# A list scheduler with other costs, a turned order inside the values operation, and new nominal places, in a fused attention and feed-forward kernel

## The chip, the core and the metric

The kernel runs on one core of a Trainium2 chip. Its engines work side by side, each through its own queue in order: TensorE (matmuls, PE in the profile), VectorE (DVE), ScalarE (ACT), GpSimd (POOL) and SyncE (SP), which issues nearly all DMA transfers. The metric is the device time of one execution in microseconds (us), lower is better.

## The reference

Eight batches, twelve heads of width 64, a sequence of 448. Attention with a sigmoid in the place of the softmax, then a mixing over the sequence of rank 32, then a feed-forward layer of width 3072:

```python
scores = scale * np.matmul(q, k.transpose(0, 1, 3, 2)) - np.log(S)
attn = 1.0 / (1.0 + np.exp(-scores))
attn_out = np.matmul(attn, v)                    # (8, 12, 448, 64)
x = attn_out.transpose(0, 2, 1, 3).reshape(B, S, 768)
h = x.transpose(0, 2, 1) @ U @ V
u = x + h.transpose(0, 2, 1)
out = u + np.maximum(u @ w_ch1, 0.0) @ w_ch2
```

## The kernel before

**Numbers.** Inputs are 64-bit floats. The weights are brought from HBM as pairs of 32-bit words and decoded on VectorE and ScalarE, then each f32 value is split into a large and a small f16 part; a product of two such values is three f16 matmuls. Batches 0 and 1 (`b < WHOLE`) do their attention in f32 instead.

**Work.** `pair(b, p, ...)` does two heads of one batch: `scores_of` (L486 on; its matmuls have L503) writes scores of four blocks of keys for two heads, each in its own bank of PSUM; `sigmoid` (L590) and the split into parts (L611 on ScalarE, L363 on VectorE) turn them into attention; `values_of` (matmuls L514 and L518) multiplies them with the values into one bank. The keys are 3 x 128 + 64. The first three blocks are done per head, with 64 columns of output each (128\*64, L518, two heads side by side in the array). The last 64 keys of both heads lie on top of each other in one block of 128 rows, so that one full matmul (128\*128, L514) does both heads. Scores use 64 rows of the array per head (64\*128, L503), again two heads side by side.

Mixing follows (`mix`, L662 to L703, for batches 0 and 1; `mix_half`, L755 and L764, for the others), then for batches 0 to 3 the feed-forward layer: `ffn_in` (18 full matmuls, L838) and `ffn_out` (12, L858), in six units per batch. Batches 4 to 7 do theirs in two pairs at the end (`in_quad`, `out_quad`, both through `product`, L1033), with seven products in the place of eight. The sums of weights for that are made on GpSimd by `quarter_sums` (L917, L921).

**Order.** Nothing of the order is written out by hand: `Plan` takes every operation with its engine, its cost, what it reads and writes, and a nominal place `pos`. `Plan.order()` simulates the engines: at each step it looks for the engine that can start something earliest, and among the operations that can start then takes the one with the lowest `pos`. An operation's start needs its inputs (`land`, `slack` and `op[5]` are latencies between engines), its engine, the port that VectorE and GpSimd share (`port`), and a free buffer for each new tile (a bank of PSUM among them: `PS_` gives batches 2 to 7 five banks for scores, values and mixing, batches 0 and 1 four; the first pairs may take all eight). The result is emitted as each engine's queue. The constants at the head of the file place the work: `START` and `ROOM0`, `ROOM` say where the feed-forward of a batch begins (`BEGIN`), `DECODE` how far ahead of its unit a weight is decoded, `BEFORE` how far ahead of batch 0's feed-forward the attention of batch 1 starts, `VALUES` and `SECOND` where a pair's values and its second scores lie, `MIX_1` and `MIX_2` the second part of the mixing, `EV_IN` and `EV_OUT` the evictions, `A_OFF` the splitting of attention, `U_AT` and `U_STEP`, `LEAD`, `SUMS`, `STEP_K`, `STEP_I` the loads and sums for the last two pairs of batches.

Of the kernel before, what the change touches and what calls it, by code (L numbers as in the profile page):

```python
# [39 lines left out]
S = 448  # L40
# [12 lines left out]
WHOLE = 2  # L53
PLAIN = 4
LATER = [2, 4, 3, 5, 6, 7]
FORMS = {1: (0,), 2: (1,), 3: (2,)}
MM = 0.190

ROOM0, ROOM, AHEAD, BEFORE, PACE = 36.845, 45.6, 45.326, 25.79, 0.913
PREP, BOUNDS, VALUES, SECOND, MIXED = 15.498, 8, 1.44, 2.168, 6.09  # L60
LOW_POOL = ()
MIXED1, MIX_1 = 6.452, 3.6
MIX_2, EV_IN, EV_OUT, A_OFF = 6.852, 20.566, 6.028, 0.0
START, DECODE = 55.894, 39.655
U_AT, U_STEP = 4.779, 4.652
LEAD, SUMS, STEP_K, STEP_I, FFN_LEAD = 30.119, 20, 24.441, 14, 4.0
ORDER = "iiiioiooiioiooiioiooiooo"


# [19 lines left out]
class Plan:  # L89
# [10 lines left out]
        self.queues.setdefault(name, []).append(t)  # L100
        return t

    def op(self, eng, cost, fn, reads=(), writes=(), pos=0.0, slack=0.0, land=0.12, after=(), port=False):
        deps = set(after)
        for k in reads:
            deps.update(self.wrote.get(k, ()))
        for k in writes:
            deps.update(self.wrote.get(k, ()))
            deps.update(self.read.get(k, ()))
        i = len(self.ops)  # L110
        for k in reads:
            self.read.setdefault(k, []).append(i)
        for k in writes:
            self.wrote[k], self.read[k] = [i], []
        tiles = []
        for k in (*reads, *writes):
            t = k[0] if isinstance(k, tuple) else k
            if isinstance(t, Tile) and t not in tiles:
                tiles.append(t)
                t.users.append(i)  # L120
                if t.at is None:
                    t.at = (pos, i)
        self.ops.append((eng, cost, fn, sorted(deps), pos, slack, land, tiles, port))
        return i

    def order(self):
        n = len(self.ops)
        left = [len(o[3]) for o in self.ops]
        users = [[] for _ in range(n)]
        for i, o in enumerate(self.ops):  # L130
            for d in o[3]:
                users[d].append(i)
        for q in self.queues.values():
            q.sort(key=lambda t: t.at)
            for t in q:
                t.left = len(t.users)
        ready, end = [0.0] * n, [0.0] * n
        free, cand = {}, {}
        for i, o in enumerate(self.ops):
            free.setdefault(o[0], 0.0)  # L140
            cand.setdefault(o[0], [])
            if not left[i]:
                cand[o[0]].append(i)
        done, port, landed = [], 0.0, [0.0] * 8

        def room(i):

            when, taken = 0.0, []
            for t in self.ops[i][7]:
                if t.got is None:  # L150
                    if t.in_turn and self.queues[t.name][0] is not t:
                        return None
                    best = None
                    for b in t.buffers:
                        if b.live or b in taken or any(x.live for x in b.shares):
                            continue
                        at = max([b.free] + [x.free for x in b.shares])
                        if best is None or at < best[0]:
                            best = at, b
                    if best is None:  # L160
                        return None
                    taken.append(best[1])
                    when = max(when, best[0])
            return when, taken

        while len(done) < n:
            best = None
            for e, c in cand.items():
                now = []
                for i in c:  # L170
                    r = room(i)
                    if r is not None:
                        o = self.ops[i]
                        now.append((max(free[e], ready[i], r[0] + o[5] if r[1] else 0.0, port if o[8] else 0.0, landed[-8] if e == "SP" else 0.0), o[4], i))
                if now:
                    t = min(now)[0]
                    if best is None or t < best[0]:
                        best = t, e, now
            if best is None:
                raise RuntimeError(f"stuck after {len(done)} of {n}")  # L180
            t, e, now = best
            i = min((x[1], x[2]) for x in now if x[0] <= t + 1e-9)[1]
            o = self.ops[i]
            taken = room(i)[1]
            for x in o[7]:
                if x.got is None:
                    x.got = taken.pop(0)
                    x.got.live = True
                    if x.in_turn:
                        self.queues[x.name].pop(0)  # L190
            cand[e].remove(i)
            end[i] = t + o[1]
            free[e] = end[i]
            if o[8]:
                port = end[i]
            if e == "SP":
                landed.append(end[i] + o[6])
            done.append(i)
            for x in o[7]:
                x.left -= 1  # L200
                x.got.free = max(x.got.free, end[i] + o[6])
                if not x.left:
                    x.got.live = False
            for u in users[i]:
                x = self.ops[u]
                at = end[i] + (o[6] + x[5] if x[0] != e or e == "SP" else 0.0 if e == "PE" else 0.06)
                ready[u] = max(ready[u], at)
                left[u] -= 1
                if not left[u]:
                    cand[x[0]].append(u)  # L210
        return done
# [9 lines left out]
def fused_kernel(ctx: ExitStack, tc: tile.TileContext, q, k, v, wu, wv, w1, w2, out):  # L221
    nc = tc.nc
    B = q.shape[0]
    plan = Plan()
    op = plan.op
# [114 lines left out]
        op("SP", max(0.6, n / 0.30e6), lambda: nc.sync.dma_start(out=dst(), in_=src()), reads, writes, pos, land=land)  # L340

    def dve(cost, fn, reads, writes, pos):
        op("DVE", cost, fn, reads, writes, pos)

    def dve2(cost, fn, reads, writes, pos):

        op("DVE", cost, fn, reads, writes, pos, port=True)

    def act(cost, fn, reads, writes, pos):
        op("ACT", cost, fn, reads, writes, pos)  # L350

    def pool(cost, fn, reads, writes, pos, after=()):
        op("POOL", cost, fn, reads, writes, pos, after=after, port=bool(reads))

    def pe(cost, fn, reads, writes, pos, slack=0.8, after=()):
        return op("PE", cost, fn, reads, writes, pos, slack, 0.3, after)

    def ts(eng, out, in_, s1, op0, s2=None, op1=None):
        kw = {} if op1 is None else {"op1": op1}
# [112 lines left out]
    values_ops, scored, summed = [], [], []  # L472
# [13 lines left out]
    def scores_of(b, js, products, kp, pos, early):  # L486


        sc = {(j, h): plan.tile("sc", BANK if early else PS_[b], False) for j in js for h in range(2)}
        n = 1 if b < WHOLE else 3  # L490

        def fn():
            for j in js:
                for i, (x, y) in enumerate(products()):
                    for h in range(2):
                        if b < WHOLE:
                            o = sc[j, h].x[:, :S] if j < 3 else sc[j, h].x[rows_of(h), :S]
                            keys = x[rows_of(h), j * P : min(S, j * P + P)]
                        else:
                            o = sc[j, h].x[:, :S]  # L500
                            first = j * P - (D if j == 3 and h else 0)
                            keys = x[rows_of(h), first : first + P]
                        nc.tensor.matmul(o, keys, y[rows_of(h)], start=i == 0, stop=i == n - 1)  # L503

        scored.append(pe(len(js) * (4 if b < WHOLE else 3) * MM + 0.2, fn, kp, list(sc.values()), pos, after=values_ops[-2:-1]))
        return sc

    def values_of(b, products, tiles, kp, pos):
        av = plan.tile("av", PS_[b], False)

        def fn():
            n = len(products())
            for i, (x, y) in enumerate(products()):
                nc.tensor.matmul(av.x[:, :S], x[:, 3, :], y(tiles[3], 0), start=i == 0, stop=False, skip_group_check=True)  # L514
            for j in range(3):
                for i, (x, y) in enumerate(products()):
                    for h in range(2):
                        nc.tensor.matmul(  # L518
                            av.x[rows_of(h), :S], x[:, j, rows_of(h)], y(tiles[j], h),
                            start=False, stop=j == 2 and i == n - 1, skip_group_check=True,  # L520
                        )

        values_ops.append(pe((16 if b < WHOLE else 12) * MM + 0.2, fn, kp, [av], pos))
        return av

    def pair(b, p, at, d):
# [406 lines left out]
    ready = {}  # L933
# [249 lines left out]
    for n, (b, g) in enumerate(slots):  # L1183
# [3 lines left out]
        at = BEGIN[b] + g * step  # L1187
# [106 lines left out]
```

## Time and profile before

| | |
|---|---|
| median of 3 runs | 1583.21 us (1581.95 to 1583.43) |
| profiled execution, from its first to its last instruction | 1581.4 us |
| TensorE matmul busy | 1561.2 us, 99%, 8774 instructions |
| VectorE busy | 1126.2 us, 71%, 1887 instructions |
| ScalarE busy | 859.8 us, 54%, 1553 instructions |
| GpSimd busy | 362.3 us, 23%, 468 instructions |
| DMA moved | 319.37 MB, 202 GB/s on average |
| granted TensorE clock, mean | 0.996 |

The profiled execution has no other time of its own beside its span; the runs lie around it and take some 1.8 us more by their median. A matmul's recorded duration (0.35 us for 448 columns) overlaps the next one; from start to start full ones follow every 0.19 us, so starts tell more than busy time.

### The profile page before, as it was taken

The numbers are of one execution on the slowest core, as the hardware profiler recorded it, in microseconds if no ns is written. First come the engines' busy times: TensorE is split into PE (matmuls) and PEld (weight loads), VectorE is DVE, ScalarE is ACT, GpSimd is POOL, SyncE is SP. The second block draws the span as 40 slices with busy tenths as digits, with TensorE's granted clock in tenths as the row PEclk, the third lists the DMA queues.
The fourth block names the chain that finished last, engine by engine and source line by source line (L and its number), as shares of the span: only waits on it lengthen the run. The fifth ranks groups of instructions, "written<-read, shape, count | busy, mean of one in ns | idle before, by whom it ended". The sixth has DMA issues, their size and how long they took to land.

```text
span 1581.4 us, 23841 instructions
## 1 busy us (share of the span) xinstructions
PE 1561.2 (99%) x8774; PEld 767.9 (49%) x8774; DVE 1126.2 (71%) x1887; ACT 859.8 (54%) x1553; POOL 362.3 (23%) x468
## 2 busy tenths in 40 slices
PE   8999998999999999999999999999999999999999
PEld 3344444544444444444444454555555555555554
DVE  3798899667767568767667677687677677565656
ACT  7667655468867757757878758332323614131210
POOL 0100002541212533312153411045543500000000
PEclk9999999999999999999999999999999999999999
DMA  8798898885565787664666584887675663333321
GB/s 248 237 308 283 277 297 261 277 267 143 151 196 142 226 256 195 183 212 97 189 225 193 167 265 162 264 268 237 216 230 181 216 225 135 124 105 133 113 105 70
DMA packets 208724, 319.37 MB, mean 202 GB/s; under 512 B 126176, under 2 KB 174688, under 8 KB 196320
## 3 DMA queue, kind: packets, MB, share of 16 engines
q1 hardware_dynamic: 208608, 317.86, 64.5%
q8 instruction: 68, 1.11, 0.3%
q14 instruction: 48, 0.39, 0.1%
HBM read 246.25 MB, written 77.42 MB: 205 GB/s over the span
## 4 chain that ended last, share of the span: by engine, by line
PE 93%; DMA 2%; DVE 2%; ACT 1%; SPq 1%; issue 0%; ACTq 0%; DVEq 0%
PE bank L1033 36%; PE bank L838 20%; PE bank L858 19%; PE bank L503 8%; PE bank L518 5%; PE bank L514 2%; PE bank L755 1%; SPq L747 1%; DMA w<-w_in 1%; DMA forms<-xnt 0%; PE bank L382 0%; DMA v__102<-v_in 0%; PE bank L764 0%; DVE stg__108 L363 0%; SPq L340 0%; DMA parked<-ub__85 0%
## 5 line engine op out<-in xcount | busy, mean ns | idle before, releaser
L858 PE MATMUL bank<-h__94,w__92 128*128 128x448 f16 x864 | 172.6, 353 | 1.3 <-DVE ua__78 L363 1.3
L858 PE MATMUL bank<-h__93,w__91 128*128 128x448 f16 x864 | 172.9, 353 | 0.0
L363 DVE SCALAR_TENSOR_TENSOR a<-at,a 128x896 f16<-128x896 f32 (+1 forms) x145 | 142.1, 988 | 32.5 <-ACT a L611 32.1
L838 PEld LDWEIGHTS <-w__89 128*128 128x128 f16 x864 | 83.5, 98 | 83.2 <-issue 7.3
L611 ACT ACTIVATE a<-at 128x896 f16<-128x896 f32 (+1 forms) x144 | 123.2, 856 | 0.7
L858 PEld LDWEIGHTS <-w__92 128*128 128x128 f16 x864 | 82.0, 98 | 84.8 <-issue 11.5
L838 PEld LDWEIGHTS <-w__90 128*128 128x128 f16 x864 | 82.9, 98 | 82.2 <-issue 8.4
L858 PEld LDWEIGHTS <-w__91 128*128 128x128 f16 x864 | 81.6, 98 | 82.5 <-issue 10.5
L1033 PEld LDWEIGHTS <-w__89 128*128 128x128 f16 x819 | 79.9, 98 | 74.6 <-issue 0.4
L1033 PEld LDWEIGHTS <-w__91 128*128 128x128 f16 x756 | 74.0, 98 | 69.0
L1033 PEld LDWEIGHTS <-w__90 128*128 128x128 f16 x756 | 74.0, 98 | 69.0
L921 POOL TENSOR_TENSOR w<-w 128x384 f32<-128x384 f32 x96 | 103.7, 1080 | 5.1
L1033 PEld LDWEIGHTS <-w__92 128*128 128x128 f16 x693 | 67.8, 98 | 63.3
L838 PE MATMUL bank<-us__87,w__89 128*128 128x448 f16 x432 | 85.2, 353 | 1.4 <-ACT h__93 L846 1.1
L838 PE MATMUL bank<-us__87,w__90 128*128 128x448 f16 x432 | 85.8, 354 | 0.6 <-DVE ua__79 L363 0.6
L838 PE MATMUL bank<-us__88,w__90 128*128 128x448 f16 x432 | 85.5, 353 | 0.0
L838 PE MATMUL bank<-us__88,w__89 128*128 128x448 f16 x432 | 85.0, 353 | 0.0
L590 ACT ACTIVATE at<-bank,bias_s,c__226 128x448 f32<-128x448 f32 (+1 forms) x96 | 67.0, 728 | 19.3 <-PE bank L503 18.7
L590 ACT ACTIVATE at<-bank,bias_s,c__225 128x448 f32<-128x448 f32 (+1 forms) x96 | 67.0, 723 | 10.7 <-PE bank L503 5.5
L590 ACT ACTIVATE at<-bank,bias_s,c__224 128x448 f32<-128x448 f32 (+1 forms) x96 | 66.9, 724 | 5.8 <-PE bank L503 4.0
L917 POOL TENSOR_TENSOR w<-w 128x384 f32<-128x384 f16 x48 | 46.0, 986 | 98.8 <-DVE xnt L925 70.0
L917 POOL TENSOR_TENSOR w<-w__89 128x384 f32<-128x384 f16 x16 | 15.2, 973 | 206.0 <-DMA forms<-scratch 178.1
(1173 smaller groups left out, 3121.7 us busy)
## 6 DMA issues: line engine op xcount, KB each, us to landing
w<-w_in SPq DMA_DIRECT2D x48, 768.0 KB, 5.9
forms<-xnt SPq DMA_DIRECT2D x24, 768.0 KB, 4.9
w__89<-forms SPq DMA_DIRECT2D x13, 1344.0 KB, 5.7
w__90<-forms SPq DMA_DIRECT2D x12, 1344.0 KB, 6.5
w__91<-forms SPq DMA_DIRECT2D x12, 1344.0 KB, 5.8
w__92<-forms SPq DMA_DIRECT2D x11, 1344.0 KB, 5.9
forms<-scratch SPq DMA_DIRECT2D x144, 96.0 KB, 4.3
w__89<-scratch SPq DMA_DIRECT2D x9, 1536.0 KB, 8.4
```

The costliest lines, as they stand in the source:

```text
L363: nc.vector.scalar_tensor_tensor(out=out, in0=in0, scalar=s, in1=in1, op0=op0, op1=op1)
L503: nc.tensor.matmul(o, keys, y[rows_of(h)], start=i == 0, stop=i == n - 1)
L514: nc.tensor.matmul(av.x[:, :S], x[:, 3, :], y(tiles[3], 0), start=i == 0, stop=False, skip_group_check=True)
L518: nc.tensor.matmul(av.x[rows_of(h), :S], x[:, j, rows_of(h)], y(tiles[j], h), start=False, stop=j == 2 and i == n - 1, skip_group_check=True,)
L590: act(cost, lambda: nc.scalar.activation(out_(), in_(), AF.Sigmoid, bias=bias_s[rows], scale=c if whole else c.x[rows]), kin + ["bias"] + ...
L611: act(0.57 if j == 3 else 0.95, lambda a=a, to=to: nc.scalar.activation(half(a, 0), to.x, AF.Copy, scale=A_UP), kto, [(a, 0)], here + A_OFF)
L747: op("SP", 1.0, lambda: nc.sync.dma_start_transpose(out=xt.x, in_=xs.x.rearrange("p c x s -> p (c x s)")), [(xs, i, x) for i in range(3) f ...
L838: nc.tensor.matmul(ph.x[:, :S], wx[:, x, c, f * P : (f + 1) * P], us.x[:, c, y, :], start=c == 0 and i == 0, stop=c == NP - 1 and i == 2,)
L858: nc.tensor.matmul(po.x[:, :S], wx[:, x, f, e * P : (e + 1) * P], h.x[:, f, y, :], start=f == 0 and i == 0, stop=f == FC - 1 and i == 2,)
L917: pool(1.0, lambda j=j: nc.gpsimd.tensor_tensor(out=t.x[:, j], in0=quarter(j, 0), in1=quarter(j, 1), op=ALU.add), [(w, j, 0), (w, j, 1)] i ...
L921: pool(1.0, lambda o_=o_, x=x, y=y, sub=sub: nc.gpsimd.tensor_tensor(out=t.x[:, o_], in0=t.x[:, x], in1=t.x[:, y], op=ALU.subtract if sub ...
L1033: nc.tensor.matmul(bank.x[:, :S], wt.x[:, k, FACTOR[n], x], both(f)[:, y], start=start and k == i == 0, stop=k == 2 and i == 2, skip_group ...
```

## The change

Four things change together.

1. In `values_of` the three half-width blocks come first and the block with the last keys, on the full array, last. The first half-width product now opens the accumulation and the last full one closes it.
2. The scheduler keeps the array's shape (`mode`). An operation on TensorE has the shape that it starts in and the one that it leaves (`modes`): (64, 64) for scores, (32, 32) for scores of batches 0 and 1 with the last keys among them, (65, 128) for values, (128, 128) for all else. A start in another shape than the last one adds `SWITCH` = 0.11 us. While the array stands in a shape other than the full one, an operation that starts in the same shape counts as 6 us earlier (`BOND`).
3. Costs on VectorE fall by 0.08 us and on ScalarE by 0.1 us, while their latency to other engines rises by as much (0.12 to 0.20 and to 0.22); a dependent operation on the same engine follows after 0.14 us where it was 0.06. A matmul is counted as 0.1893 us where it was 0.190, and scores and values get costs of their own.
4. The constants that set nominal places are new.

```diff
-MM = 0.190
-
-ROOM0, ROOM, AHEAD, BEFORE, PACE = 36.845, 45.6, 45.326, 25.79, 0.913
-PREP, BOUNDS, VALUES, SECOND, MIXED = 15.498, 8, 1.44, 2.168, 6.09
+MM = 0.1893
+SWITCH, BOND = 0.11, 6.0
+
+ROOM0, ROOM, AHEAD, BEFORE, PACE = 29.307, 45.6, 45.326, 22.996, 0.913
+PREP, BOUNDS, VALUES, SECOND, MIXED = 15.026, 7.753, 1.44, 2.168, 6.09
 LOW_POOL = ()
-MIXED1, MIX_1 = 6.452, 3.6
-MIX_2, EV_IN, EV_OUT, A_OFF = 6.852, 20.566, 6.028, 0.0
-START, DECODE = 55.894, 39.655
-U_AT, U_STEP = 4.779, 4.652
-LEAD, SUMS, STEP_K, STEP_I, FFN_LEAD = 30.119, 20, 24.441, 14, 4.0
+MIXED1, MIX_1 = 6.452, 3.7
+MIX_2, EV_IN, EV_OUT, A_OFF = 8.978, 21.237, 6.028, 1.237
+START, DECODE = 55.894, 41.023
+U_AT, U_STEP = 4.779, 4.182
+LEAD, SUMS, STEP_K, STEP_I, FFN_LEAD = 30.453, 24.808, 24.441, 12.798, 3.912
...
-        done, port, landed = [], 0.0, [0.0] * 8
+        done, port, landed, mode = [], 0.0, [0.0] * 8, 128
...
-                        now.append((max(free[e], ready[i], r[0] + o[5] if r[1] else 0.0, port if o[8] else 0.0, landed[-8] if e == "SP" else 0.0), o[4], i))
+                        bond = BOND if e == "PE" and mode != 128 and o[9][0] == mode else 0.0
+                        now.append((max(free[e], ready[i], r[0] + o[5] if r[1] else 0.0, port if o[8] else 0.0, landed[-8] if e == "SP" else 0.0), o[4] - bond, i))
...
             end[i] = t + o[1]
+            if e == "PE":
+                end[i] += SWITCH if o[9][0] != mode else 0.0
+                mode = o[9][1]
             free[e] = end[i]
...
-                at = end[i] + (o[6] + x[5] if x[0] != e or e == "SP" else 0.0 if e == "PE" else 0.06)
+                at = end[i] + (o[6] + x[5] if x[0] != e or e == "SP" else 0.0 if e == "PE" else 0.14)
...
     def dve(cost, fn, reads, writes, pos):
-        op("DVE", cost, fn, reads, writes, pos)
+        op("DVE", max(0.06, cost - 0.08), fn, reads, writes, pos, land=0.2)
...
     def act(cost, fn, reads, writes, pos):
-        op("ACT", cost, fn, reads, writes, pos)
+        op("ACT", max(0.06, cost - 0.1), fn, reads, writes, pos, land=0.22)
...
-        scored.append(pe(len(js) * (4 if b < WHOLE else 3) * MM + 0.2, fn, kp, list(sc.values()), pos, after=values_ops[-2:-1]))
+        scored.append(pe(len(js) * (0.74 if b < WHOLE else 0.57), fn, kp, list(sc.values()), pos, after=values_ops[-2:-1],
+                         modes=(64, 64) if b >= WHOLE or js[0] < 3 else (32, 32)))
...
             n = len(products())
-            for i, (x, y) in enumerate(products()):
-                nc.tensor.matmul(av.x[:, :S], x[:, 3, :], y(tiles[3], 0), start=i == 0, stop=False, skip_group_check=True)
             for j in range(3):
                 for i, (x, y) in enumerate(products()):
                     for h in range(2):
                         nc.tensor.matmul(
                             av.x[rows_of(h), :S], x[:, j, rows_of(h)], y(tiles[j], h),
-                            start=False, stop=j == 2 and i == n - 1, skip_group_check=True,
+                            start=j == 0 and i == 0, stop=False, skip_group_check=True,
                         )
-
-        values_ops.append(pe((16 if b < WHOLE else 12) * MM + 0.2, fn, kp, [av], pos))
+            for i, (x, y) in enumerate(products()):
+                nc.tensor.matmul(av.x[:, :S], x[:, 3, :], y(tiles[3], 0), start=False, stop=i == n - 1, skip_group_check=True)
+
+        values_ops.append(pe((2.97 if b < WHOLE else 2.28) + SWITCH, fn, kp, [av], pos, modes=(65, 128)))
```

More of the change, by code (lines that the diff above doesn't have):

```diff
@@ L101, in tile, with op @@
         return t
-    def op(self, eng, cost, fn, reads=(), writes=(), pos=0.0, slack=0.0, land=0.12, after=(), port=False):
+    def op(self, eng, cost, fn, reads=(), writes=(), pos=0.0, slack=0.0, land=0.12, after=(), port=False, modes=(128, 128)):
         deps = set(after)
@@ L122, in op @@
                     t.at = (pos, i)
-        self.ops.append((eng, cost, fn, sorted(deps), pos, slack, land, tiles, port))
+        self.ops.append((eng, cost, fn, sorted(deps), pos, slack, land, tiles, port, modes))
         return i
@@ L342, in dve, with pe @@
     def dve(cost, fn, reads, writes, pos):
-        op("DVE", cost, fn, reads, writes, pos)
+        op("DVE", max(0.06, cost - 0.08), fn, reads, writes, pos, land=0.2)
     def dve2(cost, fn, reads, writes, pos):
-        op("DVE", cost, fn, reads, writes, pos, port=True)
+        op("DVE", max(0.06, cost - 0.08), fn, reads, writes, pos, land=0.2, port=True)
     def act(cost, fn, reads, writes, pos):
-        op("ACT", cost, fn, reads, writes, pos)
+        op("ACT", max(0.06, cost - 0.1), fn, reads, writes, pos, land=0.22)
     def pool(cost, fn, reads, writes, pos, after=()):
         op("POOL", cost, fn, reads, writes, pos, after=after, port=bool(reads))
-    def pe(cost, fn, reads, writes, pos, slack=0.8, after=()):
-        return op("PE", cost, fn, reads, writes, pos, slack, 0.3, after)
+    def pe(cost, fn, reads, writes, pos, slack=0.8, after=(), modes=(128, 128)):
+        return op("PE", cost, fn, reads, writes, pos, slack, 0.3, after, modes=modes)
     def ts(eng, out, in_, s1, op0, s2=None, op1=None):
```

## The prediction

> **What bounds the kernel now.** I read the page first, then the busy time by stage, then the order of time on TensorE, then its waits. The page's head, its first row and the chain's shares:
>
> ```profile
> span 1581.4 us, 23841 instructions
> ...
> PE 1561.2 (99%) x8774; PEld 767.9 (49%) x8774; DVE 1126.2 (71%) x1887; ACT 859.8 (54%) x1553; POOL 362.3 (23%) x468
> ...
> PE 93%; DMA 2%; DVE 2%; ACT 1%; SPq 1%; issue 0%; ACTq 0%; DVEq 0%
> ```
>
> TensorE sets the end nearly everywhere, and the change alters no matmul's size and no count. So only time in which TensorE streams nothing can be won: stalls, stretches at half clock, and changes of the array's shape. The stages (columns: stretch, its length, then busy us and instructions of PE, PEld, DVE, ACT, POOL, then granted clock, DMA share, GB/s) say where it is:
>
> ```profile
> 0.00:40.00 40.00, 35.89 (x148) 12.73 (x149) 12.48 (x21) 28.32 (x52) 1.40 (x11) 1.00 0.81 247
> 40.00:87.00 47.00, 43.51 (x167) 15.25 (x166) 38.99 (x80) 30.70 (x63) 10.09 (x10) 0.93 0.79 247
> 87.00:205.00 118.00, 118.00 (x603) 56.27 (x602) 105.67 (x181) 81.39 (x161) 0.00 (x0) 1.00 0.87 288
> 205.00:260.00 55.00, 48.77 (x257) 25.38 (x255) 52.36 (x101) 31.79 (x64) 0.00 (x0) 0.97 0.92 310
> 260.00:310.00 50.00, 50.00 (x271) 25.40 (x269) 38.15 (x75) 18.83 (x32) 24.32 (x35) 1.00 0.78 240
> 310.00:1000.00 690.00, 687.31 (x4275) 334.11 (x4274) 488.25 (x810) 500.16 (x896) 209.49 (x298) 1.00 0.67 195
> 1045.00:1581.00 536.00, 532.74 (x2817) 275.36 (x2814) 356.15 (x562) 152.29 (x259) 110.55 (x109) 1.00 0.50 166
> ```
>
> Idle time of TensorE, length less busy: 4.1 us until 40, 3.5 in 40 to 87, none in 87 to 205, 6.2 in 205 to 260, none in 260 to 310, 2.7 in 310 to 1000, 3.3 in the last row. The first is the load of the first q and k, the last is what follows the last matmul; no edit touches either. Two stages ran below full clock: 0.07 of 47 us is 3.3 us, 0.03 of 55 us is 1.7 us. What an edit can reach is thus 3.5 + 3.3 = 6.8 us in 40 to 87, 6.2 + 1.7 = 7.9 in 205 to 260 and 2.7 in 310 to 1000: **17.4 us**, 1.1% of the span. The waits at which most of it is lost, by TensorE in order of time, and then two from the list of waits:
>
> ```profile
> 83.53 1.02 PE L514 MATMUL bank<-a,v__105 128*128 128x448 f32 x2 [1.64 <-ACT a L590]
> ...
> 253.41 0.32 PE L684 MATMUL bank<-xnt,ua 128*128 128x384 f16 x1 [1.01 <-ACT xnt L677]
> 255.71 0.32 PE L684 MATMUL bank<-xnt,ub 128*128 128x384 f16 x1 [1.98 <-DVE xnt L363]
> ```
>
> ```profile
> PE bank L755 <- ACT ub__82 L617: 1.1, 1, 1.1
> PE bank L764 <- DVE xnt L363: 0.8, 1, 0.8
> ```
>
> In 205 to 260 VectorE is the late one: it is busy 52.36 of 55 us with the last decodes, the evictions of batch 0 and the mixing of batch 1, all in one queue.
>
> **Part one: values end with the last keys.** Within a values operation (L510 to L521) the order turns round: 18 half-width matmuls first, three full ones last. What that costs is the price of changing the array's shape, from this order on TensorE:
>
> ```profile
> 321.15 1.31 PE L503 MATMUL bank<-stg__109 64*128 64x448 f16 x12
> 322.39 3.58 PE L838 MATMUL bank<-us__88,w__90 128*128 128x448 f16 x18
> 325.81 0.73 PE L514 MATMUL bank<-a,stg__108 128*128 128x448 f16 x3
> 326.47 1.89 PE L518 MATMUL bank<-a,stg__108 128*64 128x448 f16 x18
> 328.30 1.31 PE L503 MATMUL bank<-stg__109 64*128 64x448 f16 x12
> ...
> 338.63 3.57 PE L838 MATMUL bank<-us__88,w__90 128*128 128x448 f16 x18
> 342.03 4.70 PE L858 MATMUL bank<-h__93,w__91 128*128 128x448 f16 x24
> ```
>
> Starts tell the pitch: 18 full matmuls take 342.03 - 338.63 = 3.40 us, 0.189 each. Three full ones before half-width ones take 0.66 where 0.567 is streaming: 0.09 more. Twelve scores run in pairs, so 6 x 0.189 = 1.13 is streaming and 322.39 - 321.15 = 1.24 is taken: 0.11 more. So a change of shape costs **0.1 us in either direction**. A values operation between full matmuls has two changes before (full to half, half to full) and two after. Directly behind scores it had three and will have two; directly ahead of scores it had two and will have three. In batches 2 to 7, of 36 values operations, 12 stand directly ahead of scores (the first is above, 326.47 to 328.30) and 6 directly behind; the last of the former and first of the latter:
>
> ```profile
> 968.75 1.89 PE L518 MATMUL bank<-a,stg__109 128*64 128x448 f16 x18
> 970.57 1.31 PE L503 MATMUL bank<-stg__108 64*128 64x448 f16 x12
> ```
>
> ```profile
> 381.40 1.31 PE L503 MATMUL bank<-stg__108 64*128 64x448 f16 x12
> 382.64 0.74 PE L514 MATMUL bank<-a,stg__109 128*128 128x448 f16 x3
> ```
>
> With this order kept, 12 - 6 = 6 changes are added: **+0.6 us**. What a values operation adds to the changes that its neighbours have anyway is 2 between full matmuls in both orders, 2 before and 1 after where it stands behind scores, 1 before and 2 after where it stands ahead of them: 18 x 2 + 6 x 2 + 12 x 1 = 60 now. All 36 behind scores would make 36 (-2.4 us), all ahead of them 72 (+1.2 us). I take +0.6 because VALUES and SECOND, which set who stands beside whom, are untouched. The 12 values operations of batches 0 and 1 move it by 1.2 us at most. [...]
>
> BOND lets the scheduler draw scores together. In batches 2 to 7 one scores operation fills four of the five banks that scores and values share, so a second can't follow before ScalarE has emptied them: I take nothing for it there, and less than the 0.6 us above for batches 0 and 1.
>
> **Part two: occupancy apart from latency.** VectorE operations now hold their engine 0.08 us less in the plan, ScalarE's 0.1 less, with as much added before another engine may read. Does the chip do so? VectorE from 219.40, then ScalarE:
>
> ```profile
> 219.40 0.68 DVE L363 SCALAR_TENSOR_TENSOR ua__80<-bank,kg__179,ua__80 128x448 f32<-128x448 f32 x1
> 219.99 0.95 DVE L363 SCALAR_TENSOR_TENSOR stg__109<-w,stg__109 128x768 int32<-128x768 int32 x1
> 220.86 0.55 DVE L360 TENSOR_SCALAR at<-w 128x768 int32<-128x768 int32 x1
> ```
>
> ```profile
> 324.42 0.57 ACT L611 ACTIVATE a<-at 128x448 f16<-128x448 f32 x1
> 324.89 0.72 ACT L590 ACTIVATE at<-bank,bias_s,c__225 128x448 f32<-128x448 f32 x1
> ```
>
> From start to start they take 0.59, 0.87 and 0.47 us where the old plan counted 0.68, 0.97 and 0.57: the new figures (0.60, 0.89, 0.47) are the chip's. In the stage of 87 to 205 the old plan thus counted 181 x 0.08 = 14.5 us of VectorE work that wasn't there, and there VectorE indeed idles 118 - 105.67 = 12.3 us, just ahead of the stage in which TensorE waits for it. A planner that sees these 12.3 us can put decode work there (DECODE goes from 39.7 to 41.0, the step of a unit shrinks by 1/6 of the 8.1 us by which the first batch's stretch is shorter), and 6.2 us of idle need less than that. Against a full gain: DMA is at 0.87 already, and a decode needs its loads. Bounds: 0 won to all 7.9. **I take half, -3.9 us.** In 40 to 87 the chain runs through batch 0's mixing and scaling, which follow each other whatever the order; bounds 0 to 6.8, of which I take a **quarter, -1.7**. In 310 to 1000 only single waits are left, of the kind that the moved halves of mixing (MIX_2 6.9 to 9.0) and later conversions (A_OFF 1.2) address; a **third of 2.7, -0.9**.
>
> The other side of all three bounds: a new order can put fresh waits at other places, up to as much again (the third rival prices the likeliest). After 1045 the stage has no wait; LEAD, SUMS, STEP_I and FFN_LEAD change when loads and copies are due there, under cover of 0.50 DMA share and VectorE at 66%, and I cost them at nothing; uncovered, one such load late by its own time to landing (the last column) would cost 5.7 us:
>
> ```profile
> w__89<-forms SPq DMA_DIRECT2D x13, 1344.0 KB, 5.7
> ```
>
> **Sum.** -3.9 - 1.7 - 0.9 + 0.6 = **-5.9 us**: the span goes from 1581.4 to 1575.5. The median of the runs, 1583.2, lies 1.8 above the profiled span, so the time is **1577.3 us**.
>
> **Rivals.**
> *Nothing moves*: 1583 us (1580.1 to 1586.3). For it: TensorE has no idle at all in 87 to 205 and 260 to 310, and 205 to 260 has VectorE at 95% and DMA at 0.92, so decode may have nowhere to go; a stall closed at 212 reopens at 255. Then only +0.6 of the first part is left.
> *The change does not what it says*: if scores and values never come to stand otherwise and BOND never acts, the first part alone gives 1583.8. That is inside the rival above.
> *Slower, because batch 1 is ready late*. Decode is put 1.4 us sooner and batch 1's attention starts 2.8 us later (BEFORE), so both engines may work off decodes ahead of batch 1's mixing. What decides is when batch 1's split inputs are done against when TensorE wants them:
>
> ```profile
> 289.23 0.68 DVE L363 SCALAR_TENSOR_TENSOR us__88<-ub__86,s_u__177,us__88 128x448 f16<-128x448 f32 x1
> ...
> 291.12 1.11 PE L838 MATMUL bank<-us__88,w__89 128*128 128x448 f16 x5
> ```
>
> They are done at 289.91, 1.2 us before the first chain of batch 1. Later than that by more than 1.2 us against batch 0's last chain, each us costs one us; by 8 us it is 6.8, and 1583.2 + 6.8 = **1590 us**.
>
> **How the numbers follow.** Forecast 0.50, nothing moves 0.27, slower 0.23. What a measurement can tell from no change is about 0.2%, 3.2 us: faster is below 1580.0, slower above 1586.4. The forecast's own range is 1567 (nearly all 17.4 us) to 1580; taking in the other cases but the worst of the slower one, 1567 to 1589. A little of the forecast's chance lies within 0.2%, and a little of the second rival's below: 0.50, 0.27, 0.23.
>
> **What would show it.** TensorE's idle in the stretch before batch 1's first chain falls from 6.2 to about 3 us, and its granted clock rises from 0.97; VectorE's idle in the stretch ahead shrinks from 12.3. In batches 2 to 7, values show 18 half-width matmuls, then three full ones, with 0.1 us more where scores follow. Wrong would be: a first chain of batch 1 later than 291 us with split inputs that end just before it; a stage after 1045 that shows waits; or scores standing together in batches 2 to 7, which would mean that the banks allow what I excluded.

## The result

The changed kernel takes 1588.81 us by the median of 20 runs (1581.48 to 1592.72), the kernel before 1583.13 us (20 runs, 1581.83 to 1585.77). The ratio is 1.0032 with a 95% interval of 1.0024 to 1.0040: **slower by 5 us**, where 6 us faster was forecast. The runs of the changed kernel also spread over 11 us, those of the kernel before over 4. The profiled execution is one of the longer ones: its span of 1589.2 us is 7.8 us over the one of before, so its rows show some 2 us more than the medians. The spread goes with the granted clock: in the changed kernel the eight runs with a mean clock of 1.000 have a median of 1586.0 us, and the two with 0.996, of which the profiled one is one, take 1592.2 and 1592.7.

The page of the changed kernel, head, first row and shares of the chain of waits:

```profile
span 1589.2 us, 23843 instructions
...
PE 1564.5 (98%) x8774; PEld 768.4 (48%) x8774; DVE 1131.0 (71%) x1887; ACT 854.5 (54%) x1553; POOL 367.7 (23%) x468
...
PE 78%; DMA 7%; DVE 6%; issue 3%; ACT 3%; SPq 2%; POOL 1%; ACTq 0%; POOLq 0%; DVEq 0%
```

TensorE held 93% of the chain before, and DMA 2%. Idle time of TensorE went from 1581.4 - 1561.2 = 20.2 to 24.7 us, its busy time up by 3.3: together, but for rounding, the 7.8. Most lines lie 4 to 6 further down in the changed kernel: scores are L508, half-width values L522, full values L527, `ffn_in` L844, `ffn_out` L864. Its stages, with the columns of the stage rows of before:

```profile
0.00:40.00 40.00, 35.05 (x144) 13.18 (x144) 10.43 (x14) 28.20 (x52) 1.39 (x11) 1.00 0.80 235
40.00:87.00 47.00, 44.43 (x171) 15.30 (x170) 38.54 (x80) 30.03 (x60) 6.72 (x7) 0.93 0.77 250
87.00:205.00 118.00, 115.65 (x588) 54.95 (x588) 111.43 (x193) 83.28 (x168) 2.95 (x3) 1.00 0.85 288
205.00:260.00 55.00, 54.87 (x298) 28.85 (x296) 51.73 (x100) 29.07 (x57) 2.92 (x6) 1.00 0.84 279
...
310.00:1000.00 690.00, 681.03 (x4222) 329.90 (x4222) 481.68 (x798) 486.14 (x881) 206.19 (x294) 1.00 0.68 194
1000.00:1045.00 45.00, 43.71 (x242) 21.81 (x239) 28.54 (x53) 19.03 (x34) 0.64 (x1) 1.00 0.85 278
1045.00:1589.00 544.00, 539.85 (x2853) 278.88 (x2851) 366.74 (x580) 156.72 (x265) 118.87 (x114) 1.00 0.49 165
```

Length less busy gives TensorE's idle time: in 205 to 260 it fell from 6.2 to 0.1 us, and the clock rose from 0.97 to 1.00. In 87 to 205 it rose from nothing to 2.3, in **310 to 1000 from 2.7 to 9.0**, in 1000 to 1045 from nothing to 1.3. In the last row TensorE is busy 7.1 us longer than before (539.85 against 532.74): that is work which came late to 1045, not a slower tail. The waits of TensorE, longest sums first (what waits, who released it, us in all, times, the longest):

```profile
PE bank L770 <- DVE xnt L368: 4.5, 3, 2.3
PE bank L508 <- DMA qk__99<-q_in: 4.2, 1, 4.2
PE bank L522 <- ACT a L596: 3.2, 2, 2.6
PE bank L761 <- ACT at L596: 1.9, 2, 1.6
PE bank L864 <- DVE h__93 L853: 1.2, 1, 1.2
```

The second row is the first load, as before. The waits of mixing (L770, L761) in batches 2 to 7 are the new ones: 4.5 and 1.9 us, where the list of before had 0.8 and 1.1 at the same places. Behind the longest of them the granted clock is 0.57 from 827 to 831, which by an estimate, 0.43 x 4, costs 1.7 us more that counts as busy: 12 matmuls start there, and 23 in the 4 us after it.

One of them, followed back. SyncE's queue, then ScalarE, then TensorE (start, duration, engine, line, operation; in brackets the idle time ahead and what ended it):

```profile
419.55 3.88 SPq L753 DMA_TRANSPOSE w<-w  x1
...
424.17 0.53 SPq L345 DMA_DIRECT2D qk__101<-k_in  x1
```

```profile
428.57 0.58 ACT L425 ACTIVATE junk<-qk__101 128x448 bf16<-128x448 f32 x1 [6.46 <-DMA qk__101<-k_in]
...
429.85 0.53 ACT L851 ACTIVATE r__96<-bank 128x448 f32<-128x448 f32 x1
...
430.69 0.71 ACT L596 ACTIVATE at<-bank,bias_s,c__226 64x448 f32<-64x448 f32 x1
```

```profile
427.65 2.24 PE L864 MATMUL bank<-h__93,w__91 128*128 128x448 f16 x11
431.46 0.65 PE L761 MATMUL bank<-w,ua 128*128 128x384 f16 x3 [1.56 <-ACT at L596]
```

A transfer that transposes holds SyncE's queue for 3.88 us. The load of k behind it starts at 424.17 and has landed at 428.57, when ScalarE has waited 6.46 us at the head of its queue to compute the bound of that load. The relu and the sigmoid of other work stand behind it in the same queue, and TensorE runs out of work at 429.9.

The longest of these waits has the same head, here SyncE's queue, ScalarE and TensorE:

```profile
810.04 5.08 SPq L753 DMA_TRANSPOSE w<-w  x1
...
818.94 0.58 ACT L425 ACTIVATE junk<-qk__100 128x448 bf16<-128x448 f32 x1 [4.90 <-DMA qk__100<-q_in]
...
827.33 0.55 PE L770 MATMUL bank<-vst,xnt 128*128 128x448 f16 x1 [2.30 <-DVE xnt L368]
```

The next longest, 1.70 us at 614.63, goes back to another late transfer: ScalarE stood 2.10 us for `forms<-xnt`. These three are 5.6 of the 9.0 us.

### The profile page after: what moved, and what is told of

It reads as the page before. It is cut to its first block, busy times and chain, and to the rows that moved or that the text cites. A ratio compares the mean times of both kernels' runs of the same rounds, so it can differ in the third digit from the quotient of the medians.

```text
span 1589.2 us, 23843 instructions
## 1 busy us (share of the span) xinstructions
PE 1564.5 (98%) x8774; PEld 768.4 (48%) x8774; DVE 1131.0 (71%) x1887; ACT 854.5 (54%) x1553; POOL 367.7 (23%) x468
## 4 chain that ended last, share of the span: by engine, by line
PE 78%; DMA 7%; DVE 6%; issue 3%; ACT 3%; SPq 2%; POOL 1%; ACTq 0%; POOLq 0%; DVEq 0%
PE bank L1039 35%; PE bank L864 15%; PE bank L844 15%; PE bank L508 5%; PE bank L522 4%; PE bank L527 2%; DMA w<-w_in 1%; SPq L345 1%; ACT at L596 1%; DVE a L368 1%; PE bank L761 1%; DVE stg__108 L368 1%; DMA qk__101<-q_in 1%; DVE stg__109 L368 1%; ACT junk L425 1%
## 5 line engine op out<-in xcount | busy, mean ns | idle before, releaser
L864 PE MATMUL bank<-h__93,w__91 128*128 128x448 f16 x864 | 173.5, 353 | 1.2 <-DVE h__93 L853 1.2
L864 PE MATMUL bank<-h__94,w__92 128*128 128x448 f16 x864 | 173.1, 353 | 0.0
L844 PE MATMUL bank<-us__87,w__90 128*128 128x448 f16 x648 | 130.0, 355 | 0.5 <-ACT inv_w__191 L394 0.5
L844 PE MATMUL bank<-us__87,w__89 128*128 128x448 f16 x648 | 127.7, 353 | 0.6 <-DVE us__87 L368 0.4
L844 PEld LDWEIGHTS <-w__90 128*128 128x128 f16 x864 | 83.7, 98 | 84.1 <-issue 9.2
L864 PEld LDWEIGHTS <-w__91 128*128 128x128 f16 x864 | 82.8, 98 | 83.1 <-issue 8.9
L844 PEld LDWEIGHTS <-w__89 128*128 128x128 f16 x864 | 83.1, 98 | 82.2 <-issue 6.7
L864 PEld LDWEIGHTS <-w__92 128*128 128x128 f16 x864 | 82.6, 98 | 79.9 <-issue 6.6
L617 ACT ACTIVATE a<-at 128x896 f16<-128x896 f32 (+1 forms) x144 | 117.8, 856 | 0.5
L927 POOL TENSOR_TENSOR w<-w 128x384 f32<-128x384 f32 x96 | 108.4, 1129 | 5.0
L596 ACT ACTIVATE at<-bank,bias_s,c__226 128x448 f32<-128x448 f32 (+1 forms) x96 | 64.8, 721 | 18.7 <-PE bank L508 14.7
L596 ACT ACTIVATE at<-bank,bias_s,c__225 128x448 f32<-128x448 f32 (+1 forms) x96 | 65.2, 722 | 17.7 <-PE bank L508 9.3
L596 ACT ACTIVATE at<-bank,bias_s,c__224 128x448 f32<-128x448 f32 (+1 forms) x96 | 64.7, 721 | 11.5 <-PE bank L508 6.3
L596 ACT ACTIVATE a<-bank,bias_s 128x448 f32<-128x448 f32 (+1 forms) x96 | 55.1, 640 | 3.5 <-PE bank L508 2.8
L851 ACT ACTIVATE r__95<-bank 128x448 f32<-128x448 f32 x48 | 25.9, 540 | 52.9 <-PE bank L844 49.9
L365 POOL TENSOR_SCALAR inv_qkv__218<-e_qkv__215 128x3 f32<-128x3 f32 x12 | 3.8, 313 | 204.1 <-DVE e_qkv__215 L365 200.3
```

Of the source, the lines that this page charges most:

```text
L596: act(cost, lambda: nc.scalar.activation(out_(), in_(), AF.Sigmoid, bias=bias_s[rows], scale=c if whole else c.x[rows]), kin + ["bias"] + ...
L617: act(0.57 if j == 3 else 0.95, lambda a=a, to=to: nc.scalar.activation(half(a, 0), to.x, AF.Copy, scale=A_UP), kto, [(a, 0)], here + A_OFF)
L844: nc.tensor.matmul(ph.x[:, :S], wx[:, x, c, f * P : (f + 1) * P], us.x[:, c, y, :], start=c == 0 and i == 0, stop=c == NP - 1 and i == 2,)
L851: act(0.54, lambda: nc.scalar.activation(r.x, ph.x[:, :S], AF.Relu, scale=DOWN_H), [ph], [r], pos - EV_IN)
L864: nc.tensor.matmul(po.x[:, :S], wx[:, x, f, e * P : (e + 1) * P], h.x[:, f, y, :], start=f == 0 and i == 0, stop=f == FC - 1 and i == 2,)
L927: pool(1.0, lambda o_=o_, x=x, y=y, sub=sub: nc.gpsimd.tensor_tensor(out=t.x[:, o_], in0=t.x[:, x], in1=t.x[:, y], op=ALU.subtract if sub ...
```

## The experiments

All ratios are against the kernel before, run beside it. The question of the first four was which of the parts loses the time.

**The turned values order alone.** The kernel before, with only the emission inside `values_of` turned:

```diff
-            for i, (x, y) in enumerate(products()):
-                nc.tensor.matmul(av.x[:, :S], x[:, 3, :], y(tiles[3], 0), start=i == 0, ...)
             for j in range(3):
...
+            for i, (x, y) in enumerate(products()):
+                nc.tensor.matmul(av.x[:, :S], x[:, 3, :], y(tiles[3], 0), start=False, stop=i == n - 1, ...)
```

> The kernel before with only the turned order inside the values operation; every queue's order is otherwise the same. By the count of shape changes (12 values operations ahead of scores, 6 behind them in batches 2 to 7) the time rises by 0.6 us, to 1583.8, with no new wait. Rival: values now need the block that ScalarE and VectorE finish last 0.57 us sooner, and TensorE waits at the third block: more than 2 us slower, with idle time at the half-width matmuls.

Measured: 1583.89 us, ratio 0.9998 (0.9988 to 1.0009), which is -1.9 to +1.4 us. The forecast's +0.6 lies inside, and the rival's 2 us or more lies outside.

**The scheduler alone.** New costs, shapes and bond with the old places and the old order inside values:

```diff
-MM = 0.190
+MM = 0.1893
+SWITCH, BOND = 0.11, 6.0
...
-        op("DVE", cost, fn, reads, writes, pos)
+        op("DVE", max(0.06, cost - 0.08), fn, reads, writes, pos, land=0.2)
...
+        values_ops.append(pe((2.97 if b < WHOLE else 2.28) + SWITCH, fn, kp, [av], pos, modes=(128, 65)))
```

> The kernel before with only the scheduler's new costs, shapes and bond; old order of values, old nominal places. Theory A (the new costs are to blame: the 0.08 and 0.1 us were the plan's reserve for late loads and the shared port, and without it single waits come up in 310 to 1000 us): 1586 to 1590, with 5 us or more of TensorE idle in 310 to 1000. Theory B (the new places are to blame): 1578 to 1584, idle in 310 to 1000 near the 2.7 us of before.

Measured: 1601.26 us, ratio 1.0116 (1.0098 to 1.0134). Its stage row:

```profile
310.00:1000.00 690.00, 677.24 (x4177) 326.39 (x4175) 480.31 (x799) 490.26 (x889) 201.68 (x288) 0.99 0.67 189
```

12.8 us of idle time there, more than in the whole change. Prices nearer to the chip's did not by themselves make a better order on the chip.

**The places alone.** The old scheduler with the new constants:

```diff
-ROOM0, ROOM, AHEAD, BEFORE, PACE = 36.845, 45.6, 45.326, 25.79, 0.913
+ROOM0, ROOM, AHEAD, BEFORE, PACE = 29.307, 45.6, 45.326, 22.996, 0.913
...
-MIX_2, EV_IN, EV_OUT, A_OFF = 6.852, 20.566, 6.028, 0.0
+MIX_2, EV_IN, EV_OUT, A_OFF = 8.978, 21.237, 6.028, 1.237
```

> The kernel before with only the new nominal places; old costs, old order of values. Theory A: 1581 to 1585, idle in 310 to 1000 near 2.7 us. Theory B: 1587 to 1592, with 6 us or more of idle there, at the second half of the mixing.

Measured: 1620.86 us, ratio 1.0234 (1.0220 to 1.0248). Its stages:

```profile
205.00:310.00 105.00, 90.99 (x465) 46.89 (x464) 87.36 (x164) 45.06 (x85) 26.38 (x36) 0.95 0.86 272
...
1000.00:1050.00 50.00, 38.99 (x232) 16.92 (x228) 31.79 (x55) 33.35 (x53) 6.61 (x10) 0.86 0.55 181
```

14.0 us idle where the whole change has 0.2 (205 to 310), and 11.0 in 1000 to 1050. The parts do not add: +1.2% and +2.3% alone, +0.3% together. Both theories failed at this: neither had a range above 1592 for either part. The places belong to the scheduler with which they are used.

**The whole change with the old order inside values**, and the plan told so:

```diff
-        values_ops.append(pe((2.97 if b < WHOLE else 2.28) + SWITCH, fn, kp, [av], pos, modes=(65, 128)))
+        values_ops.append(pe((2.97 if b < WHOLE else 2.28) + SWITCH, fn, kp, [av], pos, modes=(128, 65)))
```

> The whole change but for the order inside values, which stays as before (the plan is told that it starts full and ends half-width). Theories A and B both: 1588, within 1.5 us of the whole change, the difference being shape changes of 0.1 us each. If it is at 1583 or below, the turned order is what costs, by another way than the count of shape changes.

Measured: 1609.97 us, ratio 1.0164 (1.0150 to 1.0178): 22 us above the 1588 that was expected. The next run shows that it isn't the matmuls: there the plan was left as the change has it, and only the emission inside values turned back.

```diff
+            for i, (x, y) in enumerate(products()):
+                nc.tensor.matmul(av.x[:, :S], x[:, 3, :], y(tiles[3], 0), start=i == 0, ...)
             for j in range(3):
...
-            for i, (x, y) in enumerate(products()):
-                nc.tensor.matmul(av.x[:, :S], x[:, 3, :], y(tiles[3], 0), start=False, stop=i == n - 1, ...)
```

> The whole change with the plan exactly as it is (it still thinks that values start half-width and end full), but the values operation written out in the old order, full block first. 17 values operations of batches 2 to 7 stand ahead of scores and 9 behind them in this plan, so the old order has 8 changes of shape less: 0.8 us faster, 1588.0. If it is at 1584 or below, the turned order itself costs; if at 1609, as with the old order told to the plan, the order on TensorE and not the plan decides.

Measured: 1588.30 us, ratio 1.0028 (1.0015 to 1.0041), as expected and as the change itself. So the 21 us of the kernel ahead of it came from another order that the plan drew, because a values operation was declared to start and end in other shapes.

**How much does one order weigh?** The change with a single figure of the plan put back:

```diff
-MM = 0.1893
+MM = 0.190
```

> The whole change with one number of the plan put back: a matmul counted as 0.190 us instead of 0.1893. No instruction changes, only the order. Theory D with nominal places that fit one single order: the plan's own end goes from 1577.7 to 1601.3, and the chip follows, 1600 or more. If places had a meaning beyond that one order, 0.0007 us per matmul would move the time by less than 3 us: 1586 to 1592.

Measured: 1616.43 us, ratio 1.0189 (1.0169 to 1.0209). By the ratios, 0.7 ns per matmul in the plan moved the chip by some 25 us (1.6%). The plan's own end had moved as far, from 1577.7 to 1601.3: the places fit one order, and the plan saw that. Its longest wait of TensorE:

```profile
PE bank L864 <- DMA w__91<-scratch: 6.7, 1, 6.7
```

A weight that is fetched late.

**Are late loads the cause?** Two ways to take them away, each done to both kernels. First the weights that batches 1 to 3 fetch, cut from 6144 columns to 64 (12,288 bytes per partition to 128), so that less is in the way of the loads there (the DMA engines' busy share in 310 to 1000 falls from 0.68 to 0.46):

```diff
-        load(lambda: w.x, lambda: scratch[i][g], P * 2 * WE * 2, [("scratch", i, g)], kw_of(w), pos)
+        load(lambda: w.x[:, 0, :64], lambda: scratch[i][g][:, 0, :64], P * 2 * WE * 2, [("scratch", i, g)], kw_of(w), pos)
```

> The whole change, with every queue's order kept, but each of the 36 fetches of scaled weights for batches 1 to 3 moves 64 columns of its 6144 (1/96 of 1536 KB; the products then use what lies in the buffer). Theory D (loads land later than the plan says, 3 to 8 us for q and k against 2.6 planned, because these transfers are in their way, and the new plan has no reserve for it): TensorE's idle in 310 to 1000 us falls from 9 to 3 us or less and the time to 1578 to 1583. Theory E (the engines' own costs are too low in the plan): the time stays at 1587 to 1590.

> The kernel before with the same 36 fetches cut to 64 columns. It has 2.7 us of idle in 310 to 1000, so under both theories at most 3 us are won: 1580 to 1583.5. If it gains as much as the change with light weights, the transfers cost both plans alike and are not what tells them apart.

Measured: the change 1581.33 us, ratio 0.9987 (0.9977 to 0.9996); the kernel before 1581.07 us, ratio 0.9987 (0.9977 to 0.9998). Idle time of TensorE in 310 to 1000 falls from 9.0 to 2.6 us in the changed kernel, and from 2.7 to nothing in the one before; their rows in that order:

```profile
310.00:1000.00 690.00, 687.42 (x4273) 334.05 (x4272) 486.84 (x806) 491.59 (x891) 204.38 (x295) 1.00 0.46 123
```

```profile
310.00:1000.00 690.00, 690.00 (x4301) 335.92 (x4299) 490.16 (x811) 501.62 (x898) 206.63 (x298) 1.00 0.46 122
```

The two kernels then take the same time: the change gains 7 us from it and the kernel before 2. In 310 to 1000 the change still idles 2.6 us more, where it was 6.3.

Second, the 12 transposing transfers replaced by plain copies of the same bytes:

```diff
-        op("SP", 1.0, lambda: nc.sync.dma_start_transpose(out=xt.x, in_=...),
+        op("SP", 1.0, lambda: nc.sync.dma_start(out=xt.x, in_=...),
```

> The whole change, orders kept, with each of the 12 transposing transfers of the mixing replaced by a plain copy of the same bytes (the mixing then sees untransposed data). A transposing transfer holds SyncE's queue for 3.2 to 6.4 us where the plan counts 1.0, and the loads of q, k and v stand behind it. Theory D in this form (the queue, not the other transfers): 1580 to 1584. If the queue is not what delays: 1587 to 1589.

> The kernel before with the 12 transposing transfers replaced by plain copies of the same bytes, orders kept (the mixing sees untransposed data). Theory D (the new plan has no reserve for SyncE's queue being held; the old one has): at most 3 us are won, 1580 to 1583.5, against 11 us in the change. Rival (the transfers hold both kernels alike, and the change is slower for another reason): 10 us or more are won here too, 1573 or less.

Measured: the change 1577.82 us, ratio 0.9967 (0.9956 to 0.9979); the kernel before 1579.98 us, ratio 0.9964 (0.9951 to 0.9976). Equal again by the ratios: the change gains 10 us from it (0.65%), the kernel before 6 us (0.36%). Both gains are larger than expected: 1580 to 1584 was the range for the change, and at most 3 us for the kernel before. So the transfers cost both kernels something, and the change more by nearly all that it is slower. Their rows, in the changed kernel, then with plain copies (duration in ns, least, median, most; then us to landing); in the kernel before they hold the queue much alike, 3157/3598/8264:

```profile
L753 SPq DMA_TRANSPOSE w<-w x12: 3202/3930/6367, 373.2 to 1032.4; - x12
...
DMA to landing us min/median/max: 5.0/6.1/8.4
```

```profile
L753 SPq DMA_DIRECT2D w<-w x12: 472/504/560, 370.4 to 1019.3; - x12
...
DMA to landing us min/median/max: 3.3/4.6/10.0
```

And the stages, the change with plain copies, then the kernel before with them:

```profile
87.00:205.00 118.00, 114.83 (x586) 54.86 (x585) 110.19 (x192) 80.86 (x163) 0.05 (x1) 1.00 0.87 294
205.00:310.00 105.00, 104.92 (x573) 54.26 (x573) 93.57 (x168) 52.38 (x102) 33.26 (x40) 1.00 0.82 268
310.00:1000.00 690.00, 689.09 (x4289) 335.08 (x4285) 490.69 (x808) 490.23 (x884) 204.28 (x293) 1.00 0.65 198
1000.00:1050.00 50.00, 48.61 (x258) 24.68 (x255) 38.16 (x77) 20.75 (x39) 0.64 (x1) 1.00 0.71 235
```

```profile
87.00:205.00 118.00, 118.00 (x602) 56.19 (x602) 105.58 (x185) 81.70 (x163) 0.00 (x0) 1.00 0.87 289
205.00:310.00 105.00, 98.18 (x517) 50.18 (x518) 88.29 (x168) 48.57 (x91) 24.28 (x35) 0.97 0.83 272
310.00:1000.00 690.00, 690.00 (x4301) 335.93 (x4299) 490.60 (x812) 500.73 (x897) 211.85 (x298) 1.00 0.64 196
```

So without the transposing transfers what is left is a near draw: the change wins 6.8 - 0.1 = 6.7 us in 205 to 310 and gives back 3.2 in 87 to 205, 0.9 in 310 to 1000 and 1.4 in 1000 to 1050.

**Is it more waiting, or less cover?** ScalarE's idle time at L425 (L420 before) in 310 to 1000, by the load that ended it (us, times), the changed kernel and then the one before:

```profile
  DMA qk__101<-k_in: 16.3, 5
  DMA qk__99<-k_in: 9.0, 5
  DMA qk__100<-q_in: 6.0, 2
```

```profile
  DMA qk__99<-k_in: 16.5, 5
  DMA qk__101<-k_in: 9.3, 4
  DMA qk__101<-q_in: 5.8, 2
```

With the smaller rows for q, k and v it is 46 us after and 41 before. ScalarE thus waited for loads nearly as long before, and TensorE lost only 2.7 us; after, it loses 9.0. Nor do the loads themselves take longer: the median from issue to landing for q and k is 3.3 to 5.1 us, by tile, in the kernel before and 3.2 to 4.6 in the changed one.

**Can the plan be told?** The change, with the transposing transfer priced as it holds the queue, and the places searched anew for that, in two versions:

```diff
-        op("SP", 1.0, lambda: nc.sync.dma_start_transpose(...), ..., pos + 1.0, land=7.0)
+        op("SP", 4.0, lambda: nc.sync.dma_start_transpose(...), ..., pos + 1.0, land=2.2)
```

The first version moves ROOM to 48.514, AHEAD to 41.784, PREP to 13.908, START to 59.111, LEAD to 31.495 and eleven more constants; the second leaves ROOM and LEAD and moves fourteen, AHEAD to 46.052, MIX_2 to 9.569 and EV_OUT to 5.318 among them. They were searched with a model in which each queue runs in order and the transfers share one path.

> The whole change with the plan told that a transposing transfer holds SyncE's queue for 4.0 us (it lands 6.2 us after its start), and nominal places searched again against an executor of the plan's queues in order, in which transfers share one path of 0.34 MB per us. Theory D: with the queue's hold known the stalls in 310 to 1000 go and the time is below both kernels, 1575 to 1581. If the chip's stalls come from elsewhere: 1585 or more, like the change.

> As the run before, from another start of the search: other places, another order, and the same end in the executor within 0.5 us. Theory D: 1575 to 1581 again. If this one is above 1585 and the other below 1581, the executor's end says little, and the first was chance.

Measured: 1582.45 us, ratio 0.9979 (0.9967 to 0.9992), and 1581.86 us, ratio 0.9980 (0.9967 to 0.9992): both faster than the kernel before by 3 us, and than the change by some 8, though both just above the 1575 to 1581 that was expected. One stage of the first:

```profile
310.00:1000.00 690.00, 689.73 (x4298) 335.84 (x4297) 493.04 (x826) 495.89 (x897) 206.38 (x295) 1.00 0.72 203
```

The 9.0 us of idle time are down to 0.3, with the transposing transfers still there. That the price and not the search alone did it is not separated by these two runs.

## Why the prediction was wrong

The forecast was -5.9 us, the time +5, a miss of some 11. Term by term:

- **205 to 260, "I take half, -3.9 us"**: the mechanism was right and the term too small. All 7.9 us came. VectorE did what the plan's prices suggested: its idle time in 87 to 205 went from 12.3 to 118 - 111.43 = 6.6 us. That the scheduler and not the places did this is shown by the runs of the parts: with the scheduler alone VectorE idles 118 - 111.95 = 6.1 us there, and TensorE 2.7 us in 205 to 310 instead of 6.2; with the places alone TensorE idles 14.0 there. The scheduler alone:

```profile
87.00:205.00 118.00, 116.29 (x586) 55.43 (x583) 111.95 (x194) 81.49 (x164) 2.25 (x3) 0.99 0.86 290
205.00:310.00 105.00, 102.26 (x551) 52.76 (x550) 93.30 (x170) 51.59 (x100) 34.21 (x43) 1.00 0.83 272
```

- **The price of that in 87 to 205 had no term.** TensorE, which had no idle time there, lost 2.3 us. Reading the stage as full of free VectorE time left out that work pulled into it stands in one queue with what TensorE needs; the wait for h__93 from VectorE (1.2 us, above) is the longest of them.
- **40 to 87, "a quarter, -1.7"**: 3.5 us of idle time became 2.6, while 0 to 40 rose from 4.1 to 4.9, so nothing came. The clock there stayed at 0.93. The edit is not all that decides it: kernels of this set whose edits lie only behind 87 us show 0.98 to 1.00 over 0 to 87 instead of 0.96. What such a clock is worth differs. In the kernel before with light weights (first row) TensorE idles 87 - 76.79 = 10.2 us instead of 7.6, and 316 matmuls fall into these 87 us instead of 313. In the changed kernel with plain copies (second row) TensorE idles 7.8 us where the changed kernel idles 7.5, and 327 matmuls fall into them instead of 314: 13 more, by an estimate at 0.19 us each some 2.5 us:

```profile
0.00:87.00 87.00, 76.79 (x316) 27.29 (x317) 52.68 (x100) 59.21 (x114) 11.47 (x21) 1.00 0.85 249
```

```profile
0.00:87.00 87.00, 79.16 (x327) 29.00 (x328) 52.44 (x101) 61.21 (x119) 11.20 (x21) 1.00 0.79 246
```

- **Part one, +0.6**: the price of a change of shape held (below), and alone it can't be told from nothing. "With this order kept" did not hold: 17 values operations in batches 2 to 7 stand ahead of scores and 9 behind, where it was 12 and 6. By the prediction's own count the 36 then add 17 x 2 + 9 x 1 + 10 x 2 = 63 changes of shape where they added 60, worth 0.3 us, so the term is small either way. That VALUES and SECOND were untouched is no ground for the order between neighbours to stay.
- **BOND "nothing" in batches 2 to 7**: right. No scores stand together there; each operation of 12 matmuls has other work on both sides.
- **310 to 1000, "a third of 2.7, -0.9": the step that failed.** It became +6.3, the largest part of the miss. I looked only at what could be won and took the single waits for the target of the moved halves. What was not read there is how much of this stage's calm was cover: ScalarE already waited 41 us for loads of q, k and v, SyncE's queue was held by 12 transposing transfers for a median of 3.6 us each, and nearly none of it reached TensorE. An order that is drawn anew in every queue puts that cover at stake, and the sum had only gains in it. The runs showed in its place: the waits for loads grew little, from 41 to 46 us, but 9.0 us of TensorE's time were lost where it had been 2.7, and without the transposing transfers 0.9. The sentence on "fresh waits at other places, up to as much again" named the risk but bounded it by the 2.7 us of waits that were visible, not by the 41 that were hidden.
- **After 1045 "nothing"**: about right for the stage itself (idle 4.1 against 3.3), but 1000 to 1045 lost 1.3.
- **The slower rival** had another mechanism, batch 1 ready late. Its 1590 us lies near the measured time, but by luck, since its condition did not come true: the first chain of batch 1 starts at 288.59, before it was 291.12:

```profile
288.59 7.73 PE L844 MATMUL bank<-us__87,w__89 128*128 128x448 f16 x40
```

What is shown: either removal of the late loads, of the weights in their way or of the transfers that hold their queue, brings the two kernels to the same time, so the 5 us lie where both reach: in transfers that come late. Neither removal is quite pure: the plain copies also land 1.5 us sooner themselves (4.6 against 6.1), and how soon the light weights themselves land was not measured. And equal does not mean that the forecast gain is then seen: most of what the change wins in 205 to 310 it gives back in the other stages. What is argued only: why the old order withstood them. By the plan's own reckoning, which is no time of a chip, the kernel before ends at 1595.0 and the changed one at 1577.7; the profiled spans are 1581.4 and 1589.2. The old prices were too high for VectorE and ScalarE (0.68 and 0.57 us for operations that take 0.59 and 0.47), so the chip ran ahead of the old plan by 14 us, and a load that the plan doesn't know to be late could be caught by that; the new plan has no such reserve. Reckoned in the same way, the kept kernels bear this out: with the old prices and the new places the plan ends at 1646.6 and the span is 1618.0, again ahead; the four plans with the new prices end 1 to 16 us before their spans; and the two with the transfer's hold priced end at 1579.8 and 1580.2, for spans of 1580.2 and 1583.6. But an order can also be good or bad by itself, by plain luck: the kernel with one figure moved by 0.7 ns loses 25 us, and none of the runs varies the reserve alone. This stays open.

## What to carry to other kernels

When a change redraws an order throughout, the waits that end on the bound engine are not the measure of the risk: look at what other engines' queues wait for and are covered against (here 41 us on ScalarE), and let the range and the chances follow that. A planner's prices that are too high may be a reserve against what it doesn't know (here it fits, and is not shown); before they are made exact, the transfers that hold a queue (here for a median of 3.9 us, where the plan counts 1.0) should be priced too. Constants that were searched for one scheduler hold for that one alone, and a sum of small gains over an order that is drawn anew says little against the scatter of such orders, from 1582 to 1621 us here.

## What the runs showed of the hardware that was not expected

A transposing transfer holds SyncE's queue for 3.2 to 6.4 us, its median 3.9, where a plain copy of the same bytes takes 0.5, and a load behind it starts only then (the hold ends at 423.43, the load starts at 424.17, above). The medians to landing are 6.1 against 4.6 us, so in this case, by the median, the transposing transfer also lands later than the plain copy.

Loads of q and k, 112 KB, take a median of 3.2 to 4.6 us from issue to landing in the changed kernel and 2.7 to 3.2 with light weights; one name of each:

```profile
qk__100<-k_in SPq DMA_DIRECT2D x32, 112.0 KB, 4.6
```

```profile
qk__100<-k_in SPq DMA_DIRECT2D x32, 112.0 KB, 2.8
```

The price of a change of the array's shape is again 0.1 us in the changed kernel: 18 half-width matmuls, with full ones on both sides, take 324.06 - 322.24 = 1.82 us where 9 x 0.189 = 1.70 is streaming, and the three full ones ahead of scores 0.68 where 0.57 is.

```profile
322.24 1.89 PE L522 MATMUL bank<-a,stg__108 128*64 128x448 f16 x18
324.06 0.74 PE L527 MATMUL bank<-a,stg__108 128*128 128x448 f16 x3
324.74 1.31 PE L508 MATMUL bank<-stg__109 64*128 64x448 f16 x12
```
